# Block attention and a wave MLP on one core: the transposed input of the last middle tile from TensorE and ScalarE, its store on two queues

## Chip, core and metric

One core of a Trainium2 chip runs the kernel. The metric is the device time of one execution in microseconds; before the change its median is 190.77 us over three runs (190.2 to 191.58).

Five engines work side by side, each on its own instructions in order: TensorE (PE in the profile; PEld are its weight loads), VectorE (DVE), ScalarE (ACT), GpSimd (POOL) and SyncE (SP). They wait for each other by semaphores. DMAs are issued from the queues of SP, ACT and POOL and run on 16 shared DMA engines. A DMA issue stands in its engine's order like any instruction: what stands behind it, or ahead of it, is held up by it or holds it up.

## What is computed

```python
# q, k, v: 8 batches, 8 heads, 576 rows, 64 columns
scores = scale * q_c @ k_c.T            # in 9 chunks of 64 rows, each on its own
attn   = softmax(scores)
x      = attn @ v_c                     # heads side by side: x is [8, 576, 512]
theta  = x @ w_theta                    # [512, 512]
y      = einsum('ts,bsd->btd', w_tok_r, x * cos(theta)) \
       + einsum('ts,bsd->btd', w_tok_i, x * sin(theta))   # [576, 576] each
u      = x + y
out    = u + max(u @ w_ch, 0)           # w_ch is [512, 512], out float32
```

## The kernel before

The eight batches are taken as four pairs p = 0 to 3. A pair has 2 x 576 rows: four full tiles of 128 rows for each batch (j = 0 to 3 and j = 4 to 7) and one middle tile, j = 8, which holds the last 64 rows of both batches (MID in the code). So there are 36 tiles. Inside, everything is in fp16, with sums in fp32 in PSUM, which is one tile of eight banks.

The program is a list of steps in one string, ORDER (lines 17 to 64). Each step is written kind.tile.slot, and the loop at line 641 emits the steps one after the other. Nothing reorders them: on every engine the instructions stand in the order of the list, and only the waits between engines are put in by the framework, from the tiles that are written and read. The two digits of a step's tile are the pair and j, so 38 is the middle tile of the last pair, and 37 is its last full tile. The number behind it is a PSUM bank or the slot of a buffer.

The steps that the last 15 us are made of:

- Y.38.4 (line 523): the token mix of tile 38 on TensorE into bank 4. A.38 (line 550): VectorE adds x to it and writes u over x. Same for the other tiles.
- ud.38.3 (line 560, the DMA at line 565): u transposed into slot 3 of buffer uT by a DMA transpose on SyncE's queue. The other way, which the kernel uses for earlier tiles, is U.xx (line 554): four TensorE transposes of 128x128 into a bank, and ua.xx (line 569): ScalarE copies the bank into a slot of uT.
- W.38.5 (line 575): four matmuls of uT with w_ch into bank 5. W0 and W1 are halves of 256 columns, used for tile 37.
- R.38.0 (line 588): VectorE takes max(.,0), adds u, and writes slot 0 of the output buffer o. R0 and R1 are the halves.
- st, sa, sg (line 600): the store of a tile from o to the output, on the queue of SyncE, ScalarE or GpSimd. A middle tile goes to two batches and so is stored by two DMAs of 64 rows (line 605); a full tile by one (line 608). sx is a kind that puts the first half on SyncE's queue and the second on ScalarE's; ORDER does not use it before the change.

A slot of a buffer is written again only when its last reader is done. For o the reader is a store, and it is done when it has landed. The slots of o at the end: R.35.1, R.33.1 and R0.37.1 follow each other in slot 1; R.31.2, R.27.2 and R1.37.2 in slot 2; R.34.0 and R.38.0 in slot 0; R.30.3 and R.24.3 in slot 3. In uT, ud.38.3 follows ud.34.3.

The last steps on each engine, in order, before the change:

- TensorE: Y.38, W.34, W.36, W.30, W.33, W.27, W.32, W.38, W.24, W0.37, W1.37
- VectorE: A.37, R.35, R.31, A.38, R.34, R.30, R.36, R.33, R.27, R.32, R.38, R.24, R0.37, R1.37
- ScalarE: sa.28 (two DMAs), sa.35, sa.34, sa.33, sa.27, sa.24, sa1.37. It has no arithmetic after 155.2 us.
- SyncE: ud.36, ud.32, ud.27, ud.37, ud.38, st.30, st.38 (two DMAs), st0.37
- GpSimd: sg.31, sg.22, sg.36, sg.32

Of the kernel before, what the change touches and what calls it, by code (L numbers as in the profile page):

```python
# [14 lines left out]


ORDER = """
pre.00 hq.0A.0 hk.0A.1 lt.00.2 cqa.0A.3 ckv.0A Tq.0A.0 init.00 Tk1.0A Tk0.0A dm.28.7
S0.0A.0 S1.0A.2 lt.01.4 qk.0M.5 E0.0A.0 v.0A dm.15.7 V0.0A.4 E1.0A Tq.0M.1 Tk.0M qk.0B.6
V1.0A.6 N0.0A S.0M.0 N1.0A cta.01 Tq.0B.2 E.0M.1 v.0M cta.00 dm.6.3 X1.0A.2 Tk0.0B  # L20
X0.0A.3 dm.2.7 S0.0B.4 Tk1.0B V0.0M.0 xa0.0A.0 V1.0M.1 xa1.0A N0.0M E0.0B.2 S1.0B.6
E1.0B H0.0A.3 v.0B V1.0B.4 G0.0A.0 V0.0B.6 lw.01.7 H1.0A.2 N1.0M N1.0B X.0M.0 xa.0M.1
lw.03.8 N0.0B TW.01.4 twv.01 X1.0B.1 X0.0B.3 lw.02.9 xv0.0B.2 lw.00.10 G1.0A Z0.0A Z1.0A
xa1.0B H.0M.6 G.0M.1 H0.0B.7 TW.03.4 G0.0B.2 H1.0B.0 twv.03 G1.0B Z.0M Z0.0B qk.0C.11
Ya.01.3 v.0C Z1.0B TW.02.1 qk.0D.12 Ya.03.6 twa.02 Tq.0C.0 TW.00.4 Ym.05.7 Tk.0C v.0D
Ya.02.0 Yb.02 twv.00 S.0C.1 Ym.02 A.02 Yb.01 E.0C.3 Ym.01 V1.0C.4 A.01 V0.0C.0 Tq.0D.1
N1.0C Yb.03 lc.00 Ya.00.2 U.02.3 Tk.0D Yb.00 Ym.00 S.0D.4 N0.0C ua.02.0 A.00 X.0C.3
U.00.0 U.01.1 Ym.03 E.0D.0 xv.0C.3 uv.01.1 V1.0D.4 ua.00.2 N1.0D V0.0D.2 N0.0D qk.1M.0
qk.1A.1 H.0C.0 v.1M qk.1B.3 A.03 v.1A Ym.06.4 X.0D.5 W.02.2 Ym.07.3 xv.0D.0 G.0C.0 Z.0C
H.0D.5 Ya.05 Ya.06 Ya.07 G.0D.1 T.1M.2 S.1M.0 T.1A.0 Z.0D R.02.0 S.1A.5 E.1A.1 Yb.05  # L30
Yb.06 Ym.04.2 A.05 E.1M.2 V0.1M.5 N0.1M qk.1D.5 V1.1M.6 V1.1A.0 A.06 N1.1M Ya.04 T.1B.1
Yb.07 U.06.7 ua.06.3 A.07 X.1M.5 Yb.04 xa.1M.1 S.1B.6 N1.1A lw.04.4 TW.04.4 twv.04
H.1M.3 A.04 v.1B V0.1A.0 E.1B.3 V1.1B.4 G.1M.2 qk.2A.2 V0.1B.6 N0.1A N0.1B N1.1B Y.08.2
A.08 X.1A.0 W.00.1 U.04.6 qk.1C.6 X.1B.7 xa.1A.2 R.00.1 qk.2M.7 Z.1M T.1D.2 xa.1B.3
qk.2B.8 v.1D U.08.3 ua.08.4 v.2M v.1C ua.04.5 H.1A.4 G.1A.0 st.02 H.1B.0 W.08.2 W.06.7
U.05.3 T.1C.0 S.1D.4 G.1B.1 qk.2C.9 Z.1A Z.1B ua.05.6 E.1D.0 S.1C.0 W.01.6 R.06.2 U.07.3
sa.06 E.1C.2 T.2A.1 ua.07.7 Y.12.7 V1.1D.4 R.01.3 V0.1D.0 Y.13.6 T.2M.2 N0.1D S.2M.0
sa.01 E.2M.1 R.08.4 N1.1D S.2A.2 V1.1C.4 E.2A.3 sa.08 V0.1C.0 A.12 Y.11.7 X.1D.2 xa.1D.0
N1.1C N0.1C X.1C.3 xv.1C.1 Y.10.4 A.13 H.1D.0 qk.3M.10 v.2B T.2C.0 A.11 A.10 T.3M.2
G.1D.2 Z.1D H.1C.2 W.04.5 R.04.5 U.03.6 W.05.7 S.2C.0 v.2A st.00 S.3M.4 uv.03.0 G.1C.0  # L40
Z.1C R.05.0 E.3M.0 v.3M E.2C.2 st.04 V1.2A.2 N1.2A W.03.6 R.03.1 T.2B.1 Y.16.7 A.16
V0.2M.4 N0.2M v.2C V1.2C.2 V1.2M.5 qk.3A.11 N1.2C S.2B.0 N1.2M E.2B.1 qk.2D.12 Y.18.6
V1.3M.7 V0.2C.0 A.18 N0.2C V0.2B.2 N0.2B Y.14.4 V1.2B.5 V0.2A.0 qk.3C.0 v.2D N1.2B
U.18.2 Y.15.3 X.2B.5 A.14 X.2M.6 W.07.4 uv.18.2 xa.2B.2 N0.2A xa.2M.3 A.15 X.2A.2 v.3B
xa.2A.0 H.2B.0 T.3C.0 R.07.2 T.2D.2 G.2B.1 qk.3B.1 W.18.3 R.18.3 H.2A.5 U.15.4 Y.17.2
U.10.3 H.2M.0 Z.2B G.2A.2 ua.15.4 ua.10.3 N1.3M G.2M.0 S.3C.5 Z.2A A.17 S.2D.3 E.2D.2
W.15.1 U.17.7 Z.2M Y.20.2 uv.17.1 V1.2D.3 E.3C.1 A.20 V0.3M.0 V0.2D.5 st.05 Y.23.7
xd.2C.1 N1.2D A.23 N0.2D T.3B.1 U.14.2 U.11.3 sa.18 N0.3M xd.2D.2 W.17.4 ua.11.5 U.16.7
R.15.4 st.07 Y.21.3 A.21 R.17.5 qk.3D.3 v.3C v.3A H.2C.5 ua.16.6 T.3A.0 W.10.7 ua.14.0
G.2C.1 T.3D.2 H.2D.0 G.2D.2 Y.22.2 Z.2C R.10.0 S.3D.3 S.3A.5 st.15 E.3A.3 S.3B.0 E.3D.0  # L50
Z.2D Y.26.7 sg.03 U.12.5 A.22 U.13.2 sa.10 ua.13.7 W.11.6 R.11.3 Y.25.3 A.26 E.3B.2 v.3D
sa.11 ud.23.2 ud.21.4 W.16.4 A.25 R.16.1 W.13.2 V1.3D.0 R.13.2 V1.3A.6 V0.3A.3 N1.3D
ua.12.1 N0.3A st.16 sa.13 xd.3M.0 N1.3A Y.24.5 A.24 Y.27.2 A.27 W.12.0 R.12.4 V0.3D.3
V1.3B.6 V0.3B.1 N1.3B xd.3A.3 ud.20.3 N0.3B N0.3D Y.28.5 V1.3C.6 V0.3C.0 A.28 W.14.2
H.3M.3 G.3M.0 R.14.0 xd.3B.1 ud.25.5 N0.3C H.3A.4 xd.3D.2 G.3A.1 W.21.2 N1.3C R.21.3
W.23.0 Z.3A H.3B.6 G.3B.2 sg.17 Z.3M ud.24.6 W.25.1 sa.21 R.23.5 xd.3C.0 H.3D.2 ud.28.7
W.20.4 H.3C.5 ud.22.1 G.3D.1 R.25.1 Z.3B Y.30.0 G.3C.0 Z.3D ud.26.0 sg.12 Z.3C Y.31.7
R.20.2 A.30 A.31 Y.36.1 Y.35.2 W.22.3 A.35 R.22.4 Y.33.5 W.28.6 A.33 Y.34.4 sg.23 A.34
ud.35.4 R.28.3 ud.31.2 W.26.0 Y.32.7 Y.37.2 W.35.3 A.36 ud.33.5 R.26.5 W.31.5 A.32 A.37
Y.38.4 ud.34.3 ud.30.1 st.26 ud.36.7 sa.20 sg.25 sa.28 R.35.1 R.31.2 ud.32.0 A.38  # L60
ud.27.4 sg.14 W.34.6 W.36.1 W.30.0 W.33.7 sg.31 sa.35 R.34.0 ud.37.2 ud.38.3 R.30.3
st.30 W.27.2 sa.34 R.36.5 sg.22 R.33.1 sg.36 R.27.2 W.32.3 R.32.4 W.38.5 R.38.0 sg.32
sa.33 sa.27 W.24.4 R.24.3 sa.24 W0.37.6 R0.37.1 st.38 W1.37.0 R1.37.2 sa1.37 st0.37
""".split()


# [611 lines left out]
```

## Time and profile before

| what | value |
|---|---|
| median of three runs | 190.77 us |
| the profiled execution, its own time | 190.93 us |
| span of its profile, first to last instruction | 189.2 us |
| granted TensorE clock, mean | 0.994 |
| stores at the end: last one issued, landed after | 184.70 us, 3.3 us |

The times in the profile count from the first instruction, so they stand against the span of 189.2 us; the execution's own time is 1.7 us longer. A row of the timeline has the start, the length, the engine, the line, the operation, what it writes and reads, its shape, and how many instructions are merged into it; brackets at its end give how long the engine was idle before and what ended that. A q behind an engine's name marks its sequencer, which issues DMAs. The length of a DMA row is that of its issue; when it landed is told by the DMA issues (line, queue, count, KB each, median us from issue to landing). Busy shares are averages over the whole span; what one change is worth is read at its place in the timeline and in the chain of work that ended last.

### The profile page before, as it was taken

The page shows a single profiled execution, that of the slowest core. Times are in us where ns is not written, and L with a number is a line of the kernel's source. Part 1 is how long each engine was busy: PE and PEld are TensorE (multiplying, and loading weights), DVE is VectorE, ACT ScalarE, POOL GpSimd, SP SyncE. Part 2 cuts the span into 40 slices and gives each one's busy share as a digit, 9 for nine tenths or more (in the row PEclk, how much of TensorE's full clock was granted, in tenths as well). Part 3 has the DMA queues.
Part 4 walks back from the last instruction along what each step waited for, and adds up shares of the span by engine and source line. Part 5 has one row for each costly group of instructions (what it writes and reads, how often), then busy time and mean ns, then how long its engine had stood idle before and what let it go on. Part 6 is the DMA issues. An engine that isn't in the chain of part 4 may idle for free.

```text
span 189.2 us, 6104 instructions
## 1 busy us (share of the span) xinstructions
PE 180.9 (96%) x2645; PEld 93.4 (49%) x2645; DVE 136.7 (72%) x259; ACT 94.8 (50%) x123; POOL 89.5 (47%) x129
## 2 busy tenths in 40 slices
PE   7998999999999999999999999999999999999970
PEld 2455555554566465545564555464554444444430
DVE  0426887889798999699887858945797963464760
ACT  3246996186566993586229966694306660000000
POOL 8765996689795885899359440100010200002010
PEclk9999999999999999999999999999999999999997
DMA  5999999999999999999999996911467851257986
GB/s 151 285 194 172 177 167 170 189 168 168 192 194 180 198 126 206 178 101 191 209 166 146 172 214 52 248 60 59 140 153 154 183 177 59 55 110 204 206 317 166
DMA packets 99227, 31.48 MB, mean 166 GB/s; under 512 B 90880, under 2 KB 94848, under 8 KB 99200
## 3 DMA queue, kind: packets, MB, share of 16 engines
q0 software_dynamic: 75952, 18.11, 99.2%
q1 hardware_dynamic: 20896, 8.92, 21.2%
q10 hardware_dynamic: 2352, 4.06, 6.7%
q8 instruction: 20, 0.33, 0.7%
q14 instruction: 7, 0.06, 0.1%
HBM read 33.06 MB, written 9.44 MB: 225 GB/s over the span
## 4 chain that ended last, share of the span: by engine, by line
PE 74%; DMA 17%; DVE 3%; issue 2%; POOL 2%; SPq 0%; DVEq 0%; POOLq 0%
PE psum L540 34%; PE psum L475 15%; PE psum L580 12%; DMA land<-in_k_dram 9%; PE psum L354 4%; PE psum L400 3%; DMA land<-in_q_dram 3%; DMA uT<-x 3%; PE psum L437 2%; PE psum L557 2%; DMA v<-in_v_dram 2%; PE psum L287 2%; POOL v L213 1%; DVE o L592 1%; DVE T L335 1%
## 5 line engine op out<-in xcount | busy, mean ns | idle before, releaser
L213 POOL DMA_DIRECT2D v<-in_v_dram x56 | 41.7, 765 | 14.5 <-DMA land<-in_k_dram 9.1
L540 PEld LDWEIGHTS <-wT 128*128 128x128 f16 (+1 forms) x360 | 30.6, 100 | 33.4 <-issue 0.8
L540 PE MATMUL psum<-zr,wT 128*128 128x512 f16 (+1 forms) x180 | 45.4, 381 | 0.1
L540 PE MATMUL psum<-zi,wT 128*128 128x512 f16 (+1 forms) x180 | 43.1, 379 | 0.0
L608 POOL DMA_DIRECT2D out_dram<-o x10 | 5.5, 552 | 66.3 <-DVE o L592 46.2
L580 PE MATMUL psum<-wch,uT 128*128 128x512 f16 (+1 forms) x148 | 35.2, 374 | 1.1 <-DMA uT<-x 1.1
L552 DVE TENSOR_TENSOR x<-psum,x 128x512 f16<-128x512 f32 x36 | 24.4, 683 | 15.8 <-PE psum L540 15.1
L475 PE MATMUL psum<-wtheta,xT 128*128 128x512 f16 x144 | 34.1, 379 | 0.0
L592 DVE SCALAR_TENSOR_TENSOR o<-psum,x 128x512 f32<-128x512 f32 (+1 forms) x37 | 24.3, 670 | 10.3 <-PE psum L580 6.2
L494 ACT ACTIVATE cos<-psum,pihalf 128x1024 f16<-128x1024 f32 (+1 forms) x22 | 21.2, 964 | 16.1 <-PE psum L475 16.1
L335 DVE STREAM_TRANSPOSE T<-land 64x256 f32<-64x256 f32 (+3 forms) x38 | 27.0, 725 | 2.6 <-DMA land<-in_k_dram 2.3
L417 DVE TENSOR_TENSOR x<-psum,recip 128x512 f16<-128x512 f32 (+1 forms) x40 | 25.5, 638 | 1.4
L383 ACT ACTIVATE eT<-psum 128x1024 f16<-128x1024 f32 (+1 forms) x22 | 18.4, 864 | 15.8 <-PE psum L354 15.8
L580 PEld LDWEIGHTS <-uT 128*128 128x128 f16 x148 | 13.7, 98 | 16.2 <-DMA uT<-x 1.6
L475 PEld LDWEIGHTS <-xT 128*128 128x128 f16 x144 | 13.5, 98 | 15.3 <-DVE xT L460 0.2
L143 ACT ACT_TABLE_LOAD x14 | 18.0, 1283 | 4.1 <-DVE recip L415 3.1
L494 ACT ACTIVATE sin<-psum 128x1024 f16<-128x1024 f32 (+1 forms) x22 | 19.1, 870 | 0.0
L173 POOL DMA_DIRECT2D land<-in_q_dram x15 | 13.6, 904 | 4.8 <-DVE recip L415 2.1
L157 PE MATMUL psum<-zeros 128*128 128x512 f16 x51 | 14.1, 436 | 1.2 <-DVE pihalf L148 1.2
L173 POOL DMA_DIRECT2D land<-in_k_dram x15 | 13.5, 902 | 2.0 <-DMA land<-in_k_dram 1.4
L462 ACT COPY xT<-psum 128x512 f16<-128x512 f16 (+1 forms) x11 | 8.4, 784 | 10.4 <-PE psum L437 10.4
L354 PEld LDWEIGHTS <-T 32*64 32x64 f16 x1152 | 10.6, 105 | 5.4 <-DVE T L335 2.1
(40 smaller groups left out, 140.9 us busy)
## 6 DMA issues: line engine op xcount, KB each, us to landing
land<-in_q_dram POOLq DMA_DIRECT2D x15, 256.0 KB, 6.8
land<-in_k_dram POOLq DMA_DIRECT2D x15, 256.0 KB, 7.8
out_dram<-o ACTq DMA_DIRECT2D x12, 256.0 KB, 3.2
v<-in_v_dram POOLq DMA_DIRECT2D x40, 64.0 KB, 6.2
out_dram<-o POOLq DMA_DIRECT2D x10, 256.0 KB, 3.4
out_dram<-o SPq DMA_DIRECT2D x9, 256.0 KB, 3.3
v<-in_v_dram POOLq DMA_DIRECT2D x16, 128.0 KB, 7.7
land<-in_moe_w_theta_dram SPq DMA_DIRECT2D x2, 512.0 KB, 7.6
```

Source lines behind the costliest of these rows:

```text
L173: nc.gpsimd.dma_start(t[:, w].rearrange("p h s d -> p h (s d)"), ap[2 * p + bb, :, s0 : s0 + GT, :].rearrange("h (p s) d -> p h (s d)", s=2),)
L213: nc.gpsimd.dma_start(v16[rows, slot + t, :, 0:D], v[b, :, t0 : t0 + m, :].rearrange("h s d -> s h d"),)
L335: nc.vector.transpose(to.bitcast(FP32).rearrange("p (x l s) -> p x s l", l=32, s=2), src.bitcast(FP32).rearrange("p (x s d) -> p x s d", s ...
L354: nc.tensor.matmul(ps[half[rows], r, h - hs[0]], t[quarter[c], 1, h, :, e], t[quarter[c], 0, h, :, e], start=(e == 0), stop=(e == 1), tile ...
L383: nc.scalar.activation(out=to, in_=ps, func=AF.Exp, scale=scale)
L417: nc.vector.tensor_tensor(out=x.rearrange("p r (h d) -> p r h d", h=H // 2), in0=ps[:, :, :, 0:D], in1=recip[:, 0:n].broadcast_to((P, n, H ...
L475: nc.tensor.matmul(ps[:, (j - js[0]) * DM : (j - js[0] + 1) * DM], xT[:, j, a, :], wtheta16[:, a, :], start=(a == 0), stop=(a == NDB - 1),)
L494: nc.scalar.activation(out=t[:, js[0] : js[-1] + 1].rearrange("p j e -> p (j e)"), in_=ps, func=AF.Sin, bias=bias, scale=1.0,)
L540: nc.tensor.matmul(ps[half[c]] if j == MID else ps, wT[:, kt, t0 : min(t0 + P, S)], z, start=(b is not None and i == 0), stop=(i == len(kt ...
L552: nc.vector.tensor_tensor(out=x, in0=st.pop(("ps_y", p, j)), in1=x, op=ALU.add)
L580: nc.tensor.matmul(ps, uT[:, a, :], wch16[:, a, cols[f]], start=(a == 0), stop=(a == NDB - 1),)
L592: nc.vector.scalar_tensor_tensor(out=o, in0=ps, scalar=0.0, in1=st["x", p][:, j, cols[f]], op0=ALU.max, op1=ALU.add,)
```

## The change

Four steps of ORDER differ. ud.38.3 goes; U.38.2 (four transposes into bank 2) and ua.38.3 (ScalarE's copy into the same slot of uT) come in ahead of W.30, which is also ahead of sa.35 on ScalarE. st.38 goes; sx.38 comes in ahead of W.24 in the list, with the first half on SyncE's queue and the second on ScalarE's, behind sa.27 and ahead of sa.24. All else is the same; the string is wrapped anew, so line numbers are three less from there on. The core of the diff, with the list's lines as they are wrapped:

```diff
...
-ud.27.4 sg.14 W.34.6 W.36.1 W.30.0 W.33.7 sg.31 sa.35 R.34.0 ud.37.2 ud.38.3 R.30.3
-st.30 W.27.2 sa.34 R.36.5 sg.22 R.33.1 sg.36 R.27.2 W.32.3 R.32.4 W.38.5 R.38.0 sg.32
-sa.33 sa.27 W.24.4 R.24.3 sa.24 W0.37.6 R0.37.1 st.38 W1.37.0 R1.37.2 sa1.37 st0.37
...
+Y.37.2 W.35.3 A.36 ud.33.5 R.26.5 W.31.5 A.32 A.37 Y.38.4 ud.34.3 ud.30.1 st.26 ud.36.7 sa.20
+sg.25 sa.28 R.35.1 R.31.2 ud.32.0 A.38 ud.27.4 sg.14 W.34.6 W.36.1 U.38.2 ua.38.3 W.30.0 W.33.7
+sg.31 sa.35 R.34.0 ud.37.2 R.30.3 st.30 W.27.2 sa.34 R.36.5 sg.22 R.33.1 sg.36 R.27.2 W.32.3
+R.32.4 W.38.5 R.38.0 sg.32 sa.33 sa.27 sx.38 W.24.4 R.24.3 sa.24 W0.37.6 R0.37.1 W1.37.0 R1.37.2
+sa1.37 st0.37
```

More of the change, by code (lines that the diff above doesn't have):

```diff
@@ L17 @@
 ORDER = """
[L18 to L59, printed above, removed]
@@ L60 @@
-Y.38.4 ud.34.3 ud.30.1 st.26 ud.36.7 sa.20 sg.25 sa.28 R.35.1 R.31.2 ud.32.0 A.38
-ud.27.4 sg.14 W.34.6 W.36.1 W.30.0 W.33.7 sg.31 sa.35 R.34.0 ud.37.2 ud.38.3 R.30.3
-st.30 W.27.2 sa.34 R.36.5 sg.22 R.33.1 sg.36 R.27.2 W.32.3 R.32.4 W.38.5 R.38.0 sg.32
-sa.33 sa.27 W.24.4 R.24.3 sa.24 W0.37.6 R0.37.1 st.38 W1.37.0 R1.37.2 sa1.37 st0.37
+pre.00 hq.0A.0 hk.0A.1 lt.00.2 cqa.0A.3 ckv.0A Tq.0A.0 init.00 Tk1.0A Tk0.0A dm.28.7 S0.0A.0
+S1.0A.2 lt.01.4 qk.0M.5 E0.0A.0 v.0A dm.15.7 V0.0A.4 E1.0A Tq.0M.1 Tk.0M qk.0B.6 V1.0A.6 N0.0A
@@ new lines @@
+S.0M.0 N1.0A cta.01 Tq.0B.2 E.0M.1 v.0M cta.00 dm.6.3 X1.0A.2 Tk0.0B X0.0A.3 dm.2.7 S0.0B.4
+Tk1.0B V0.0M.0 xa0.0A.0 V1.0M.1 xa1.0A N0.0M E0.0B.2 S1.0B.6 E1.0B H0.0A.3 v.0B V1.0B.4 G0.0A.0
+V0.0B.6 lw.01.7 H1.0A.2 N1.0M N1.0B X.0M.0 xa.0M.1 lw.03.8 N0.0B TW.01.4 twv.01 X1.0B.1 X0.0B.3
+lw.02.9 xv0.0B.2 lw.00.10 G1.0A Z0.0A Z1.0A xa1.0B H.0M.6 G.0M.1 H0.0B.7 TW.03.4 G0.0B.2 H1.0B.0
+twv.03 G1.0B Z.0M Z0.0B qk.0C.11 Ya.01.3 v.0C Z1.0B TW.02.1 qk.0D.12 Ya.03.6 twa.02 Tq.0C.0
+TW.00.4 Ym.05.7 Tk.0C v.0D Ya.02.0 Yb.02 twv.00 S.0C.1 Ym.02 A.02 Yb.01 E.0C.3 Ym.01 V1.0C.4
@@ new lines @@
+A.01 V0.0C.0 Tq.0D.1 N1.0C Yb.03 lc.00 Ya.00.2 U.02.3 Tk.0D Yb.00 Ym.00 S.0D.4 N0.0C ua.02.0
+A.00 X.0C.3 U.00.0 U.01.1 Ym.03 E.0D.0 xv.0C.3 uv.01.1 V1.0D.4 ua.00.2 N1.0D V0.0D.2 N0.0D
+qk.1M.0 qk.1A.1 H.0C.0 v.1M qk.1B.3 A.03 v.1A Ym.06.4 X.0D.5 W.02.2 Ym.07.3 xv.0D.0 G.0C.0 Z.0C
+H.0D.5 Ya.05 Ya.06 Ya.07 G.0D.1 T.1M.2 S.1M.0 T.1A.0 Z.0D R.02.0 S.1A.5 E.1A.1 Yb.05 Yb.06
+Ym.04.2 A.05 E.1M.2 V0.1M.5 N0.1M qk.1D.5 V1.1M.6 V1.1A.0 A.06 N1.1M Ya.04 T.1B.1 Yb.07 U.06.7
+ua.06.3 A.07 X.1M.5 Yb.04 xa.1M.1 S.1B.6 N1.1A lw.04.4 TW.04.4 twv.04 H.1M.3 A.04 v.1B V0.1A.0
@@ new lines @@
+E.1B.3 V1.1B.4 G.1M.2 qk.2A.2 V0.1B.6 N0.1A N0.1B N1.1B Y.08.2 A.08 X.1A.0 W.00.1 U.04.6 qk.1C.6
+X.1B.7 xa.1A.2 R.00.1 qk.2M.7 Z.1M T.1D.2 xa.1B.3 qk.2B.8 v.1D U.08.3 ua.08.4 v.2M v.1C ua.04.5
+H.1A.4 G.1A.0 st.02 H.1B.0 W.08.2 W.06.7 U.05.3 T.1C.0 S.1D.4 G.1B.1 qk.2C.9 Z.1A Z.1B ua.05.6
+E.1D.0 S.1C.0 W.01.6 R.06.2 U.07.3 sa.06 E.1C.2 T.2A.1 ua.07.7 Y.12.7 V1.1D.4 R.01.3 V0.1D.0
+Y.13.6 T.2M.2 N0.1D S.2M.0 sa.01 E.2M.1 R.08.4 N1.1D S.2A.2 V1.1C.4 E.2A.3 sa.08 V0.1C.0 A.12
+Y.11.7 X.1D.2 xa.1D.0 N1.1C N0.1C X.1C.3 xv.1C.1 Y.10.4 A.13 H.1D.0 qk.3M.10 v.2B T.2C.0 A.11
@@ new lines @@
+A.10 T.3M.2 G.1D.2 Z.1D H.1C.2 W.04.5 R.04.5 U.03.6 W.05.7 S.2C.0 v.2A st.00 S.3M.4 uv.03.0
+G.1C.0 Z.1C R.05.0 E.3M.0 v.3M E.2C.2 st.04 V1.2A.2 N1.2A W.03.6 R.03.1 T.2B.1 Y.16.7 A.16
+V0.2M.4 N0.2M v.2C V1.2C.2 V1.2M.5 qk.3A.11 N1.2C S.2B.0 N1.2M E.2B.1 qk.2D.12 Y.18.6 V1.3M.7
+V0.2C.0 A.18 N0.2C V0.2B.2 N0.2B Y.14.4 V1.2B.5 V0.2A.0 qk.3C.0 v.2D N1.2B U.18.2 Y.15.3 X.2B.5
+A.14 X.2M.6 W.07.4 uv.18.2 xa.2B.2 N0.2A xa.2M.3 A.15 X.2A.2 v.3B xa.2A.0 H.2B.0 T.3C.0 R.07.2
+T.2D.2 G.2B.1 qk.3B.1 W.18.3 R.18.3 H.2A.5 U.15.4 Y.17.2 U.10.3 H.2M.0 Z.2B G.2A.2 ua.15.4
@@ new lines @@
+ua.10.3 N1.3M G.2M.0 S.3C.5 Z.2A A.17 S.2D.3 E.2D.2 W.15.1 U.17.7 Z.2M Y.20.2 uv.17.1 V1.2D.3
+E.3C.1 A.20 V0.3M.0 V0.2D.5 st.05 Y.23.7 xd.2C.1 N1.2D A.23 N0.2D T.3B.1 U.14.2 U.11.3 sa.18
+N0.3M xd.2D.2 W.17.4 ua.11.5 U.16.7 R.15.4 st.07 Y.21.3 A.21 R.17.5 qk.3D.3 v.3C v.3A H.2C.5
+ua.16.6 T.3A.0 W.10.7 ua.14.0 G.2C.1 T.3D.2 H.2D.0 G.2D.2 Y.22.2 Z.2C R.10.0 S.3D.3 S.3A.5 st.15
+E.3A.3 S.3B.0 E.3D.0 Z.2D Y.26.7 sg.03 U.12.5 A.22 U.13.2 sa.10 ua.13.7 W.11.6 R.11.3 Y.25.3
+A.26 E.3B.2 v.3D sa.11 ud.23.2 ud.21.4 W.16.4 A.25 R.16.1 W.13.2 V1.3D.0 R.13.2 V1.3A.6 V0.3A.3
@@ new lines @@
+N1.3D ua.12.1 N0.3A st.16 sa.13 xd.3M.0 N1.3A Y.24.5 A.24 Y.27.2 A.27 W.12.0 R.12.4 V0.3D.3
+V1.3B.6 V0.3B.1 N1.3B xd.3A.3 ud.20.3 N0.3B N0.3D Y.28.5 V1.3C.6 V0.3C.0 A.28 W.14.2 H.3M.3
+G.3M.0 R.14.0 xd.3B.1 ud.25.5 N0.3C H.3A.4 xd.3D.2 G.3A.1 W.21.2 N1.3C R.21.3 W.23.0 Z.3A H.3B.6
+G.3B.2 sg.17 Z.3M ud.24.6 W.25.1 sa.21 R.23.5 xd.3C.0 H.3D.2 ud.28.7 W.20.4 H.3C.5 ud.22.1
+G.3D.1 R.25.1 Z.3B Y.30.0 G.3C.0 Z.3D ud.26.0 sg.12 Z.3C Y.31.7 R.20.2 A.30 A.31 Y.36.1 Y.35.2
+W.22.3 A.35 R.22.4 Y.33.5 W.28.6 A.33 Y.34.4 sg.23 A.34 ud.35.4 R.28.3 ud.31.2 W.26.0 Y.32.7
```

## The prediction

> **What bounds the kernel now.** I read the page's busy shares first, then the chain of work that ended last, then the timeline of TensorE and of the queues from 172 us on, and last the DMA issues with their times to landing.
>
> ```profile
> PE 180.9 (96%) x2645; PEld 93.4 (49%) x2645; DVE 136.7 (72%) x259; ACT 94.8 (50%) x123; POOL 89.5 (47%) x129
> ...
> PE 74%; DMA 17%; DVE 3%; issue 2%; POOL 2%; SPq 0%; DVEq 0%; POOLq 0%
> ```
>
> TensorE is busy for 96% of the span, so a gain must take work from it or close one of its few gaps. Its last gap is in the end of the chain (start, length, what):
>
> ```profile
> 176.01 5.32 DMA uT<-x
> 181.33 0.05 issue
> 181.37 1.91 PE psum L580 x8
> 183.29 0.02 issue
> 183.31 0.06 DVE o L592
> 183.37 0.39 issue
> 183.76 0.05 DVEq L592
> 183.81 0.11 issue
> 183.92 0.41 DVE o L592
> ```
>
> The transfer is ud.38, the DMA transpose that the change removes: issued at 176.01, landed at 181.33. TensorE starts W.38 0.04 us later. The timeline of TensorE gives the size of the gap:
>
> ```profile
> 174.92 5.35 PE L580 MATMUL psum<-wch,uT 128*128 128x512 f16 x24
> 181.37 2.77 PE L580 MATMUL psum<-wch,uT 128*128 128x512 f16 x16 [1.10 <-DMA uT<-x]
> ```
>
> The 24 matmuls are W.34, W.36, W.30, W.33, W.27, W.32, four each. The 16 are W.38, W.24 and the halves of W.37. The row of 24 lasts 5.35 us with 0.38 for the last matmul, so the matmuls follow each other every 0.216 us. Without a wait W.38 would start at 174.92 + 24 x 0.216 = 180.11: the wait moves it by 1.26 us. The last rows of the kernel are the two halves of tile 37: R1.37 and its store sa1.37.
>
> ```profile
> 184.25 0.42 DVE L592 SCALAR_TENSOR_TENSOR o<-psum,x 128x256 f32<-128x256 f32 x1
> 184.70 0.41 ACTq L608 DMA_DIRECT2D out_dram<-o  x1
> out_dram<-o ACTq DMA_DIRECT2D x1, 128.0 KB, 3.3
> ```
>
> So the end is 184.70 + 3.3 = 188.0 and then 1.2 us of closing to 189.2. Whatever moves R1.37 moves the end.
>
> **The change, part by part. U.38 on TensorE.** Four transposes of 128x128 are added between W.36 and W.30. No row shows them at that place; U steps elsewhere do (two U steps in one row, the matmul behind them, and the copy on ScalarE):
>
> ```profile
> 127.41 0.61 PE L557 MATMUL psum<-id,x 128*128 128x128 f16 x8
> 127.86 1.03 PE L580 MATMUL psum<-wch,uT 128*128 128x512 f16 x4
> 128.06 0.59 ACT L569 COPY uT<-psum 128x512 f16<-128x512 f16 x1 [0.80 <-PE psum L557]
> ```
>
> Eight take 127.86 - 127.41 = 0.45, so four take 0.23 us. U.38 starts after W.36, at 174.92 + 8 x 0.216 = 176.65. It needs x of tile 38 from A.38:
>
> ```profile
> 175.03 0.69 DVE L552 TENSOR_TENSOR x<-psum,x 128x512 f16<-128x512 f32 x1 [1.38 <-PE psum L540]
> ```
>
> That ends at 175.72, 0.9 before it is needed, and bank 2 was last read by A.37, before A.38. So no wait. W.30, W.33, W.27 and W.32 each start 0.23 later.
>
> **ua.38 on ScalarE.** In the row above the copy starts 0.65 us after the first transpose of its row of eight, which is 0.42 for a row of four; it lasts 0.59. So it runs from 177.07 to 177.66. W.27 needs bank 2 back at 174.92 + 16 x 0.216 + 0.23 = 178.61: 0.95 to spare. W.38 can start at 180.11 + 0.23 = 180.34: 2.7 to spare. TensorE gains 181.37 - 180.34 = 1.03 us, if nothing else holds it. The banks of W.38, W.24 and W.37 were read out before 178.7 (R.30 is the last of them), so no bank does.
>
> **What is queued behind ua.38.** ScalarE's queue is in order, and behind ua.38 stands sa.35, the store of tile 35, which did not have to wait for TensorE before. These are the stores on that queue now, with VectorE's R.33 and R.27:
>
> ```profile
> 172.82 0.34 ACTq L608 DMA_DIRECT2D out_dram<-o  x1
> ...
> 176.72 0.37 ACTq L608 DMA_DIRECT2D out_dram<-o  x1
> ...
> 179.64 0.34 ACTq L608 DMA_DIRECT2D out_dram<-o  x1
> ...
> 180.23 0.34 ACTq L608 DMA_DIRECT2D out_dram<-o  x1
> ```
>
> ```profile
> 178.92 0.68 DVE L592 SCALAR_TENSOR_TENSOR o<-psum,x 128x512 f32<-128x512 f32 x1
> ...
> 179.52 0.68 DVE L592 SCALAR_TENSOR_TENSOR o<-psum,x 128x512 f32<-128x512 f32 x1
> ```
>
> They are sa.35, sa.34, sa.33, sa.27; then R.33, R.27. A DMA that stands behind a ScalarE instruction is issued 0.07 us after that one starts:
>
> ```profile
> 147.92 1.11 ACT L494 ACTIVATE cos<-psum,pihalf 128x1024 f16<-128x1024 f32 x1 [1.43 <-PE psum L475]
> 147.99 0.34 ACTq L608 DMA_DIRECT2D out_dram<-o  x1
> ```
>
> So sa.35 goes from 172.82 to 177.14, 4.3 us later, and sa.34 follows at about 177.5 instead of 176.72. This has a price, through the output buffers. R.35.1 and R.33.1 share o slot 1, so R.33 may not write before sa.35 has landed. R0.37.1 uses that slot again and waits for sa.33; R1.37.2 uses slot 2 and waits for sa.27. The landing times of sa.35, of sa.34, and of sa.33 with sa.27, in this order:
>
> ```profile
> out_dram<-o ACTq DMA_DIRECT2D x1, 256.0 KB, 2.6
> ...
> out_dram<-o ACTq DMA_DIRECT2D x1, 256.0 KB, 4.4
> ...
> out_dram<-o ACTq DMA_DIRECT2D x2, 256.0 KB, 3.4
> ```
>
> Before, sa.35 landed at 175.4, 3.5 us ahead of R.33. Now its landing is bounded by 2.6 (its own row) and 4.4 (sa.34, issued nearly at the new moment, but beside ud.38, which is gone). I take 2.6: beside it only ud.37 is left. It lands at 179.75 and R.33 starts at 179.8, where TensorE and R.36 alone would allow 178.92 + 0.23 = 179.15.
>
> sa.27 is issued 180.23 - 178.92 = 1.31 after R.33 starts, so at 181.1. Its landing is bounded by 2.6 and 3.4. The stretches of the DMA engines tell why it took 3.4 (last two columns: share and GB/s):
>
> ```profile
> 178.40:179.00 0.60, 0.60 (x4) 0.28 (x3) 0.60 (x3) 0.00 (x0) 0.00 (x0) 1.00 0.24 9
> 179.00:180.30 1.30, 1.27 (x6) 0.39 (x4) 1.20 (x3) 0.00 (x0) 0.54 (x1) 1.00 1.02 200
> 180.30:183.40 3.10, 2.03 (x11) 1.06 (x12) 1.47 (x3) 0.00 (x0) 0.54 (x1) 1.00 1.05 408
> ```
>
> While the two late transposes hung, only 9 GB/s moved, and then the stores filled the engines at 408 GB/s for 3 us. After the change half of that jam is gone, but sa.35's 256 KB are added, so I take the middle, 3.0: sa.27 lands at 184.1. R1.37 then starts at 184.1 instead of 184.25, where TensorE alone would allow about 184.25 - 1.03 = 183.2. The ring of output buffers hands back 0.9 of the 1.03.
>
> The Trainium skill (DMA: Bandwidth & Descriptors, Anatomy of one DMA) fits 2.0 us plus bytes over 436 GB/s to a DMA. By it a 256 KB store is an estimated 2.6 us, as sa.35's row has it and the 3.4 and 4.4 rows do not; the second rival is the case in which the trace would agree with it.
>
> **The store in two halves.** The two halves of st.38 leave one queue, and st0.37 stands behind them:
>
> ```profile
> 183.17 1.19 SPq L605 DMA_DIRECT2D out_dram<-o  x2
> 184.46 0.53 SPq L608 DMA_DIRECT2D out_dram<-o  x1
> ```
>
> Moved to ScalarE's queue, the second half costs it about 0.6 us (1.19 / 2) between sa.27 and sa.24. R.38 ends 0.6 before R.24 on VectorE (the distance of R.33 and R.27), so sa.24 goes when R.24 is done, within 0.1. SyncE's queue gets 0.6 us back ahead of st0.37, which started 0.13 after R0.37's end (183.92 + 0.41). That isn't the last store; sa1.37 is. I cost this part at nothing, from -0.1 (st0.37) to +0.1 (sa.24 pushing sa1.37). The Trainium skill (DMA: Bandwidth & Descriptors, Issuing engines are not separate DMA queues) says that issuing from several engines saves the sequencer's issue time alone; the 0.6 is that, and by it too the sum stays.
>
> **ud.38 off SyncE's queue.** Behind it stands st.30, which waits for R.30 anyway (at 178.44, 0.9 after ud.38's issue ended). It moves with R.30 by 0.23: nothing. POOL's queue (sg.36, sg.32) moves with VectorE and ends before the others. No instruction ahead of W.34 is changed.
>
> **The sum** on the profiled execution: TensorE -1.26 + 0.23 = -1.03; ring of buffers +0.88; store 0; last landing 3.3 as before. That is -0.15: 190.93 - 0.15 = 190.8 there. The median of the runs, 190.77, is 0.16 below the profiled run, so 190.6.
>
> **The rivals.** (1) The gain reaches the end. For: landings of 2.4 to 2.6 where the engines are free (sa.35, and the jam is smaller). R.33 goes at 179.5, sa.27 at 180.8, lands at 183.3; R1.37 gains 0.95. Against: seven stores of 256 KB in 5 us. 189.8.
> (2) Every store lands unloaded, 2.6 for 256 KB (sa.35's row) and 2.4 for the last one, the least that a store on SyncE's queue took (st.26's row):
>
> ```profile
> out_dram<-o SPq DMA_DIRECT2D x1, 256.0 KB, 2.4
> ```
>
> R1.37 starts at 179.8 + 1.31 + 2.6 = 183.7, 0.55 earlier, and the last landing is 0.9 shorter: 189.3. Against: sa.33 and sa.27 at 3.4, sa1.37 at 3.3. The skill's fit, above, is the page that speaks for it.
> (3) Slower: sa.35 is late. With 4.4 us it lands at 181.55; R.33 starts then, sa.27 goes at 182.86 and lands, by 3.4, at 186.25: R1.37 is 2.0 later, 192.8; with 3.4 and 3.4 it is 1.0 later, 191.8. It decides from a landing of about 2.8 on (179.95 + 1.31 + 3.0 = 184.26, where it was). For: sa.34 at 176.72. Against: ud.38, the later of two transposes beside that store, is gone.
> (4) W.38 still waits, because U.38 or ua.38 does. For it A.38 would have to be 0.9 late, or the copy 2.7. Then the time is 190.8 or more.
>
> **How the numbers follow.** Forecast 0.5; rival 1 0.23; rival 2 0.07; rival 3 0.17; rival 4 0.03. The predicted time is the forecast's, 190.6. Its own part runs from 190.2 to 191.2. The range goes from 189.5 (inside rival 1, above rival 2) to 192.2 (the middle of rival 3) and leaves out 2 in 10. A measurement of this kernel can tell about 1% (1.9 us) from no change. Faster by that means under 188.9: below every case, 0.03. Slower means above 192.7: the top of rival 3, 0.05. Within 1%: 0.92.
>
> **What would show it.** Right: no TensorE gap ahead of W.38, and W.38 starting near 180.3; four L557 rows near 176.65 and one copy near 177.1; sa.35 at about 177.1 behind it; a VectorE gap of 0.3 to 1.0 ahead of R.33; another gap ahead of the halves of R.37, ended by the landing of sa.33 or sa.27 and not by TensorE. Wrong: R.33 starting at 179.15 with sa.35 landed (rival 1), all landings under 2.7 (rival 2), R.33 after 180.3 (rival 3), a gap ahead of W.38 (rival 4). The whole working would fall if something ahead of 174.9 moved.

## The result, and the profile after

The changed kernel takes 192.2 us (median; 191.66 to 193.66) against 190.68 before: a ratio of 1.0086 with a 95% interval of 1.0057 to 1.0115, or 1.1 to 2.2 us slower. The forecast was 190.6 and no measurable change. The time is within 1% of before, as forecast, but the change can be measured: the interval is 0.3% to either side, where the prediction had taken 1%.

The profiled execution took 193.66 us, the longest of the changed kernel's, with a span of 191.6. Its times are best read from the start of W.34, the first of the last matmuls, which lies at 174.92 before and at 177.28 here. This is TensorE's timeline after (start, length, operation, count), from W.34 on:

```profile
177.28 1.90 PE L577 MATMUL psum<-wch,uT 128*128 128x512 f16 x8
179.02 0.39 PE L554 MATMUL psum<-id,x 128*128 128x128 f16 x4
179.24 6.22 PE L577 MATMUL psum<-wch,uT 128*128 128x512 f16 x32
```

The gap ahead of W.38 is gone: after the four transposes 32 matmuls run without a stop, and W.30 starts 1.96 after W.34, as the prediction's 176.65 + 0.23 has it (176.88 is 1.96 after 174.92). From W.34 to the end, however, it takes 191.64 - 177.28 = 14.36 us, against 14.24 before; this stretch is called the tail from here on. The copy and the first store behind it, in ScalarE's timeline:

```profile
179.44 0.58 ACT L566 COPY uT<-psum 128x512 f16<-128x512 f16 x1 [21.95 <-PE psum L554]
179.50 0.34 ACTq L605 DMA_DIRECT2D out_dram<-o  x1
```

sa.35 is issued 2.22 after W.34 (prediction: 177.14, the same 2.22) instead of 2.10 ahead of it. It lands 3.0 us later:

```profile
out_dram<-o ACTq DMA_DIRECT2D x1, 256.0 KB, 3.0
```

VectorE shows who waits for that: R.34, then R.30 and R.36, then R.33 and all that follow.

```profile
178.35 0.69 DVE L589 SCALAR_TENSOR_TENSOR o<-psum,x 128x512 f32<-128x512 f32 x1 [0.27 <-PE psum L577]
180.30 1.29 DVE L589 SCALAR_TENSOR_TENSOR o<-psum,x 128x512 f32<-128x512 f32 x2 [1.26 <-PE psum L577]
182.57 3.97 DVE L589 SCALAR_TENSOR_TENSOR o<-psum,x 128x512 f32<-128x512 f32 x7 [0.98 <-DMA out_dram<-o]
```

R.33 starts 5.29 after W.34 (4.00 before), behind a gap of 0.98 that a store ends, not TensorE. R.33 and the six behind it then stand in one row, with TensorE ahead of them.

The chain of work that ended last runs the same way, from the transposes to the copy, ScalarE's queue, a store and VectorE:

```profile
179.18 0.24 PE psum L554 x4
...
179.44 0.02 ACT uT L566
...
179.50 0.34 ACTq L605
...
179.93 3.11 DMA out_dram<-o
...
183.18 2.26 DVE o L589 x4
...
185.57 0.43 DVE o L589
...
186.11 0.42 DVE o L589
```

The chain takes the later store, sa.34 (issued at 179.93), because a wait for it stands in VectorE's stream and came last. VectorE's own rows show that the block had begun at 182.57, with the landing of sa.35 at 182.45; sa.34 landed at 183.04, in time for R.38 at 184.4. R1.37 starts at 186.11, 8.84 after W.34 (9.33 before). The last three stores, sa.24, st0.37 and sa1.37, took 3.1, 3.1 and 3.3 us to land before; the first two take longer now:

```profile
out_dram<-o ACTq DMA_DIRECT2D x1, 256.0 KB, 3.3
out_dram<-o SPq DMA_DIRECT2D x1, 128.0 KB, 3.6
out_dram<-o ACTq DMA_DIRECT2D x1, 128.0 KB, 3.3
```

So the last landing is 12.6 after W.34, against 13.1 in the first profile of before.

There is one more thing at the very end that the prediction does not have. Behind the last landing SyncE passes its closing waits one by one. The last five of them, before and after (count, durations, first and last start):

```profile
L673 SPq EVENT_SEMAPHORE  x5: 28/28/28, 188.0 to 188.3; - x5
```

```profile
L670 SPq EVENT_SEMAPHORE  x5: 28/28/28, 190.0 to 190.7; - x5
```

Five waits that passed in 0.3 us now take 0.7, though no landing is left to wait for: the last one is at 189.9. Between the second and the third SyncE stands still for 0.46 us. The span ends 1.74 us after the last landing, before 1.17.

### The profile page after: what moved, and what is told of

Same layout as the page of the kernel before. It is cut to its first block, busy times and chain, and to the rows that moved or that the text cites. A ratio compares the mean times of both kernels' runs of the same rounds, so it can differ in the third digit from the quotient of the medians.

```text
span 191.6 us, 6113 instructions
## 1 busy us (share of the span) xinstructions
PE 181.1 (95%) x2649; PEld 93.5 (49%) x2649; DVE 136.9 (71%) x259; ACT 95.5 (50%) x124; POOL 89.5 (47%) x129
## 4 chain that ended last, share of the span: by engine, by line
PE 73%; DMA 12%; DVE 6%; POOL 4%; issue 2%; ACTq 0%; DVEq 0%; POOLq 0%; ACT 0%
PE psum L537 33%; PE psum L472 15%; PE psum L577 11%; DMA v<-in_v_dram 7%; DMA land<-in_k_dram 4%; PE psum L351 4%; PE psum L397 3%; DVE o L589 2%; PE psum L434 2%; PE psum L554 2%; POOL land L165 2%; DMA out_dram<-o 2%; PE psum L284 2%; DVE T L332 1%; DVE x L549 1%
## 5 line engine op out<-in xcount | busy, mean ns | idle before, releaser
L566 ACT COPY uT<-psum 128x512 f16<-128x512 f16 x15 | 8.5, 592 | 32.5 <-PE psum L554 31.5
L472 PEld LDWEIGHTS <-xT 128*128 128x128 f16 x144 | 13.5, 98 | 15.2 <-DVE xT L457 0.2
L577 PEld LDWEIGHTS <-uT 128*128 128x128 f16 x148 | 13.8, 98 | 14.6 <-issue 0.4
L170 POOL DMA_DIRECT2D land<-in_q_dram x15 | 13.8, 918 | 3.8 <-DVE x L414 1.3
L170 POOL DMA_DIRECT2D land<-in_k_dram x15 | 13.8, 918 | 1.3 <-DMA land<-in_k_dram 0.7
```

The lines of the kernel that those rows point to most:

```text
L170: nc.gpsimd.dma_start(t[:, w].rearrange("p h s d -> p h (s d)"), ap[2 * p + bb, :, s0 : s0 + GT, :].rearrange("h (p s) d -> p h (s d)", s=2),)
L472: nc.tensor.matmul(ps[:, (j - js[0]) * DM : (j - js[0] + 1) * DM], xT[:, j, a, :], wtheta16[:, a, :], start=(a == 0), stop=(a == NDB - 1),)
L577: nc.tensor.matmul(ps, uT[:, a, :], wch16[:, a, cols[f]], start=(a == 0), stop=(a == NDB - 1),)
```

## The experiments

All times are medians of runs on the same chip beside runs of the kernel before (191.3 to 191.45 us there, so ratios are compared). "After W.34" means after the start of the first matmul of W.34. Where a run is set beside the changed kernel, its ratio is set beside the 1.0061 of the changed kernel's second run, unless another is named. That run and the three experiments behind it were on one chip, all later ones on another.

**The changed kernel again.** No edit.

> The changed kernel, unaltered, for a second profile and more times. Its first profile starts W.34 at 177.28 us, 2.36 later than before (174.92), though no instruction ahead of W.34 differs; from W.34 to the end of the span it takes 14.3, before 14.2. Theory A (the loss is in the tail: ua.38 holds sa.35 up, sa.35 holds R.33 up, and so on to the halves of tile 37; the 2.36 us are chance): W.34 starts at 174.9 plus or minus 0.8 here, and R.33 again starts about 5.3 after W.34 with a gap of 0.7 to 1.3 ahead of it. Theory B (the loss lies ahead of W.34 and comes with the changed program): W.34 starts 1 us or more late again, and the tail is as long as before. Time 191.7 to 192.7 in both.

Measured: 192.34 us, ratio 1.0061 (1.0034 to 1.0088). W.34 started at 177.24, as late as in the first profile; R.33 5.13 after W.34 with a gap of 0.82; tail 14.4. The tail answers theory A, the start of W.34 theory B. The start alone does not settle it: both profiled executions were the longest of their kernel (193.49 here, of 191.34 to 193.49), so their late start need not be that of the median run.

**sa.35 ahead of the copy.**

```diff
-W.34.6 W.36.1 U.38.2 ua.38.3 W.30.0 W.33.7 sg.31 sa.35
+W.34.6 W.36.1 sa.35 U.38.2 ua.38.3 W.30.0 W.33.7 sg.31
```

> The changed kernel with sa.35 moved ahead of U.38 and ua.38 in the list, so that ScalarE issues it as early as before. Theory A: sa.35 starts about 2.1 before W.34, R.33 has no gap ahead of it and starts 4.2 after W.34; the halves of tile 37 start 0.4 to 1.0 earlier than in the changed kernel; time 0.5 to 1.2 below the changed kernel, 191.0 to 191.7. Theory B: R.33's gap goes too, but the time is within 0.3 of the changed kernel's. Theory C (the second half of the store on ScalarE's queue makes the end late): within 0.3 of the changed kernel.

Measured: 191.93 us, ratio 1.0026 (1.0000 to 1.0053), 0.35% below the changed kernel; the two intervals overlap, and the medians differ by 0.4 us where theory A expected 0.5 to 1.2. VectorE:

```profile
178.86 3.28 DVE L589 SCALAR_TENSOR_TENSOR o<-psum,x 128x512 f32<-128x512 f32 x5 [1.26 <-PE psum L577]
```

R.30 to R.32 run as a block of five again. W.34 starts at 175.84, so R.33 starts 4.23 after it, R1.37 8.41 (8.84 in the changed kernel), and the tail is 13.8 instead of 14.4. Theory A holds for 0.5 us of the tail. It isn't all: the kernel is still not faster than before.

**Only the transposes and the copy; the store as before.**

```diff
-sa.33 sa.27 sx.38 W.24.4 R.24.3 sa.24 W0.37.6 R0.37.1 W1.37.0
+sa.33 sa.27 W.24.4 R.24.3 sa.24 W0.37.6 R0.37.1 st.38 W1.37.0
```

> The changed kernel with tile 38 stored as before, both halves on SyncE's queue (only the transposes and the copy are new). Theory C: 0.4 to 1.2 faster than the changed kernel, near 191.0 to 191.8. Theory A: within 0.3 of the changed kernel, 192.0 to 192.5. Theory B: within 0.3 as well.

Measured: 192.57 us, ratio 1.0086 (1.0052 to 1.0120), as slow as the changed kernel or slower; tail 14.9. Theory C falls. The loss comes with the transposes, the copy and the removal of ud.38. In the tail the store in halves even gains here: without it st0.37 is issued behind both halves of tile 38 and lands last, 13.1 after W.34, where the changed kernel's last landing is at 12.6. This is one profile against two, and the time does not tell the two apart.

**Only the store in two halves.**

```diff
-sa.33 sa.27 W.24.4 R.24.3 sa.24 W0.37.6 R0.37.1 st.38 W1.37.0
+sa.33 sa.27 sx.38 W.24.4 R.24.3 sa.24 W0.37.6 R0.37.1 W1.37.0
```

> The kernel before with only the store of tile 38 in two halves on two queues. Theory A: within 0.3 of before, 190.4 to 191.0. Theory C: 0.4 to 1.2 slower than before, 191.1 to 191.9. Theory B (any change of the program moves the part ahead of W.34): W.34 starts late and the time rises by 0.5 or more.

Measured: 190.81 us, ratio 0.9977 (0.9957 to 0.9998). This half of the change does no harm. Its profile brought the next question: W.38, which still waits for ud.38 here, started only 5.63 after W.34, not 6.45.

**The kernel before again.** No edit.

> The kernel before, unaltered, for a second profile. Theory F (the first profile of before was not a usual one: ud.38 landed unusually late, so removing it is worth less than 1.03): W.38 starts 5.4 to 5.9 after W.34 instead of 6.45, and from W.34 to the end of the span it takes 13.3 to 13.9 instead of 14.2. If the first profile was usual, W.38 starts 6.3 to 6.6 after W.34 and the tail is 14.1 to 14.4. The first matmul of W.34 starts between 174.5 and 177 by chance. Time within 0.4 of before.

Measured: 191.0 us, ratio 0.9989 (0.9959 to 1.0019). TensorE from W.34 on:

```profile
175.84 5.35 PE L580 MATMUL psum<-wch,uT 128*128 128x512 f16 x24
181.38 2.77 PE L580 MATMUL psum<-wch,uT 128*128 128x512 f16 x16 [0.19 <-DMA uT<-x]
```

The same gap that took 1.10 us in the first profile takes 0.19 here. W.38 starts 5.54 after W.34, where 24 matmuls without a wait end at 5.19: removing ud.38 is worth 0.35 less the 0.23 of the transposes. The tail is 13.34, not 14.24: W.38 is 0.91 earlier and the tail 0.90 shorter. Theory F holds.

**A longer stream for SyncE.**

```diff
-sa.06 ... sa.01 ... sa.08
+st.06 ... st.01 ... st.08
```

> The changed kernel with three early stores (tiles 06, 01, 08) issued by SyncE instead of ScalarE, which makes SyncE's stream some instructions longer; nothing after 110 us differs. In the four kernels without ud.38 SyncE stops for 0.43 us among its closing waits, always behind the same number of its instructions, and the end comes 1.74 after the last landing; in the two with ud.38 it comes 1.17 after. Theory D (the stop sits at a fixed place of SyncE's stream, which is shorter without ud.38): the stop moves ahead to where SyncE waits for a landing anyway, the end comes 1.2 after the last landing, time 0.3 to 0.7 below the changed kernel. Theory A alone, without D: the end stays 1.74 after the last landing and the time is within 0.3 of the changed kernel's.

Measured: 191.67 us, ratio 1.0023 (0.9997 to 1.0050), 0.38% below the changed kernel, with overlapping intervals. R.33 still waits (5.21 after W.34), and the tail is 13.9 instead of 14.4. SyncE's stop of 0.46 us is there, but further ahead: it ends at 187.51, and the last landing is at 187.47, so it hides behind that. The span ends 1.36 after the last landing. Counted in the trace, it again stands behind the 79th instruction of SyncE, as in every other kernel that shows it. SyncE has 87 instructions in the changed kernel, 91 in this one and in the kernel before.

**A shorter stream for SyncE, ud.38 kept.** An edit of the kernel before.

```diff
-st.02 ... st.00 ... st.04
+sa.02 ... sa.00 ... sa.04
```

> The kernel before with three early stores (tiles 02, 00, 04) issued by ScalarE instead of SyncE, so that SyncE's stream is about as short as in the changed kernel, with ud.38 still there. Theory D: a stop of 0.4 appears among SyncE's closing waits, the end comes 1.6 to 1.8 after the last landing instead of 1.17, time 0.2 to 0.7 above before. If the stop belongs to the absence of ud.38 and not to the length of the stream: the end stays 1.17 after the last landing, time within 0.3 of before.

Measured: 191.05 us, ratio 0.9998 (0.9968 to 1.0028). The closing waits:

```profile
L670 SPq EVENT_SEMAPHORE  x5: 28/28/28, 187.9 to 188.6; - x5
```

The stop is there behind the 79th of 87 instructions, with ud.38 in place, and the span ends 1.65 after the last landing. So the stop goes with the length of SyncE's stream and not with ud.38, as theory D has it. The time does not show it: the interval takes in a rise of 0.5 us, but the median does not rise, and the expected 0.2 to 0.7 is not shown. What the three stores moved to ScalarE give back is not known.

**A slot of its own for R.33.**

```diff
-R.33.1
+R.33.6
```

> The changed kernel with R.33 writing a slot of its own in the output buffer, so that it need not wait for sa.35; sa.35 stays behind ua.38. Theory A: no gap ahead of R.33, which starts 4.2 after W.34 instead of 5.1 to 5.3; R1.37 starts 0.3 to 0.6 earlier (8.3 to 8.5 after W.34 instead of 8.7 to 8.8); time 0.2 to 0.8 below the changed kernel. If the late sa.35 costs in another way than through slot 1 (the stores crowd at the end): R1.37 moves by less than 0.2 and the time stays within 0.3.

Measured: 191.52 us, ratio 1.0017 (0.9990 to 1.0044), 0.44% below the changed kernel, with overlapping intervals. sa.35 stays behind the copy, and still:

```profile
179.38 3.28 DVE L589 SCALAR_TENSOR_TENSOR o<-psum,x 128x512 f32<-128x512 f32 x5 [1.26 <-PE psum L577]
```

With W.34 at 176.36 R.33 starts 4.23 after it and R1.37 8.42, as with sa.35 ahead; the tail is 13.9. It is slot 1 through which the late store costs: freeing the slot gives the same R.33, R1.37 and tail as issuing sa.35 early.

**Both costs taken away.** The changed kernel with sa.35 ahead of U.38 and the three early stores on SyncE's queue.

> The changed kernel with sa.35 ahead of U.38 and ua.38, and with three early stores on SyncE's queue: the late R.33 and the stop among the closing waits are both taken away, the transposes and the copy stay. Theory A with D and F: R.33 starts 4.2 after W.34, the last landing is 12.0 to 12.2 after W.34, the end 1.2 to 1.4 behind it; the tail of 13.2 to 13.6 is that of the kernel before in its usual state (13.34 in its second profile), so the time is within 0.3% of before. If the removal of ud.38 is worth its 1.0 us once those two are gone: 0.4% or more faster than before. If a further loss belongs to the transposes or lies ahead of W.34: 0.3% or more slower.

Measured: 190.80 us, ratio 0.9970 (0.9943 to 0.9997). VectorE has no gap ahead of R.33 (the row starts with R.30 and R.36):

```profile
178.86 3.28 DVE L589 SCALAR_TENSOR_TENSOR o<-psum,x 128x512 f32<-128x512 f32 x5 [1.26 <-PE psum L577]
```

R.33 starts 4.23 after W.34, the last landing is 12.3 after it (12.0 to 12.2 was expected), and the span ends 1.24 behind that; tail 13.5. Once more:

> The kernel with both costs of the change taken away, once more, because it came out 0.3% faster than before with an interval that almost reaches 1. If that holds, the ratio is 0.995 to 0.999; if it was chance, 0.999 to 1.002. R.33 starts 4.2 after W.34, the end comes 1.2 to 1.4 after the last landing.

Measured: 190.87 us, ratio 0.9982 (0.9951 to 1.0014), tail 13.1. The transposes with both costs off are no slower than the kernel before, and 0.2 to 0.3% faster at the medians; one of the two intervals includes 1. Both runs also have the store in halves, whose ratio alone was 0.9977, so no gain is shown for the transposes. Both intervals lie below those of the changed kernel (from 1.0034 and 1.0057 on): the two edits together take the whole loss away, which neither does clearly in time alone.

**The store in halves again.**

> The kernel before with only the store of tile 38 in two halves on two queues, once more, to see whether its 0.2% holds: R.38's two halves start together, st0.37 is no longer behind two issues; last landing 12.0 to 12.2 after W.34, ratio 0.996 to 1.000. If the 0.2% was chance, the ratio is 1.000 or above.

Measured: 191.45 us, ratio 0.9983 (0.9953 to 1.0014). The ratio is 0.2% below 1 again, but the median is not below the 191.36 of the runs beside it: a gain of 0.2% cannot be told from none.

**The kernel before, a third time.**

> The kernel before, a third profile. Theory F: W.38 starts 5.5 to 6.2 after W.34 (5.54, 5.63 and 6.20 in the other three kernels that keep ud.38, 6.45 in the first profile, 5.19 without a wait). A start of 6.4 or more would make the first profile the usual one. Ratio 0.998 to 1.002.

Measured: 191.32 us, ratio 0.9990 (0.9967 to 1.0013). The gap ahead of W.38 is so small that the 40 matmuls stand in one row:

```profile
176.37 8.27 PE L580 MATMUL psum<-wch,uT 128*128 128x512 f16 x40
```

It takes 8.27; the changed kernel takes 8.18 for the same 40 with the transposes among them (from 177.28 to 179.24 + 6.22). W.38 starts 5.50 after W.34. In the six profiles that keep ud.38 it starts at 5.35, 5.50, 5.54, 5.63, 6.20 and 6.45; the one on which the prediction was built is the last.

## Why the prediction was wrong, point by point

**The size of the wait.** "The wait moves it by 1.26 us" was read rightly from one profile and was the longest of six. In the two other profiles of the same kernel it is 0.35 and 0.31. So the gain of TensorE was not 1.03 but about 0.1. This is the first term of the sum that failed, by its size and not by its mechanism: where W.38 was 0.91 later, the tail was 0.90 longer. About 0.1 holds for the two usual profiles; two of the six start W.38 late, and against the mean of all six, 5.78, the 5.41 of the changed kernel is a gain of 0.4. The wait varied from 0.16 to 1.26 us over the six profiles, while the 24 matmuls ahead of it took 5.35 us in each profile that shows them as one row.

**U.38 and ua.38.** Right in place and size: 0.22 us of TensorE, copy 2.16 after W.34, no wait for A.38, for bank 2 or for a slot.

**sa.35 behind the copy, and the ring of output buffers.** Right as a mechanism: sa.35 2.22 after W.34, the gap ahead of R.33, the store that ends it. The sizes were off both ways: sa.35 took 2.95 to land and not 2.6, and R.33 started at 5.29 instead of 4.88; sa.27 took 2.1 and not 3.0, so R1.37 started at 8.84 instead of 9.18. That it costs is shown twice in the tail, by moving sa.35 and by freeing the slot: 0.5 us each time. In time the two are 0.35% and 0.44% below the changed kernel, each by itself at the edge of what the runs can tell. The forecast had charged 0.88 for the ring against a gain of 1.03; against a gain of 0.1, the 0.5 that it cost is nearly all loss.

**ud.38 off SyncE's queue.** "It moves with R.30 by 0.23: nothing" missed the second lost term. SyncE has 87 traced instructions instead of 91; three of the four went with ud.38 (88 with the transposes alone) and one with the second half of the store (90 with that alone). With that, a stop of 0.46 us comes to stand behind the last landing. In the kernels with 88 or 87 the span ends 1.65 to 1.78 after the last landing, in those with 90 or 91 it ends 1.17 to 1.36 after it. In the kernel before a wait for a landing stands in that place, so whether the stop is there too, hidden, can only be inferred. That it stands at a fixed place of the stream is shown by its moving along when the stream is made longer or shorter, with ud.38 and without. In the tail it costs 0.57. In time the kernel with the longer stream points to it (0.38% below the changed one, with overlapping intervals); the one with the shorter stream does not. No run moves the early stores without moving the stop, so what these moves do to the time by themselves is not known.

**The store in two halves.** Forecast at nothing, between -0.1 and +0.1; the ratios are 0.2% below 1 in both trials, one interval just below 1 and one not. The sign was within reach, the size is at the edge of what can be told.

**The sum as it is.** In the tail: 13.3 (the kernel before in its second profile), + 0.5 (ring), + 0.57 (stop), less 0.1 (TensorE) is 14.3; 14.4 was seen in both profiles of the changed kernel. That is + 1.0 us of the 1.2 to 1.6 us that the two ratios give (0.61% and 0.86%); 1.0 lies inside the interval of the second (0.65 to 1.7 us) and just below that of the first (1.1 to 2.2 us). From the changed kernel's tail of 14.4, taking the ring's cost away leaves 13.8 and 13.9, hiding the stop 13.9, and both 13.5 and 13.1, so the two add up. Rival 3 named the right side and the right queue, but its price of 1.0 to 2.0 came from a landing of 3.4 to 4.4 that did not occur; that the loss came out near it is chance.

**What stays open.** W.34 started at 177.28 and 177.24 in the two profiles of the changed kernel and between 174.92 and 176.37 in the kernels that keep ud.38. Nothing ahead of W.34 differs. About half of the 2.36 us between the first profiles of before and after is one gap on TensorE. It is shown here after and in the second profile of the kernel before; the first has none:

```profile
94.08 0.41 PE L537 MATMUL psum<-zi,wT 128*64 128x512 f16 x2 [1.09 <-issue]
```

```profile
92.64 0.41 PE L540 MATMUL psum<-zi,wT 128*64 128x512 f16 x2 [0.48 <-issue]
```

The gap is always ahead of the same matmul: 1.09 and 1.25 us in the two profiles of the changed kernel, 0.12 to 0.92 in nine others, none in three. What it waits for is not shown. In the other kernels with the transposes W.34 starts between 174.94 and 176.36, as without them, so nothing ahead of W.34 belongs to the transposes as such. Whether the changed kernel itself has a little of it in its median run is not known: 0.2 to 0.6 us of its loss are not accounted for by the tail, or are noise.

## What to carry to other kernels

A gain that is the length of a wait for a DMA should be read from more than one execution before it is booked; the length of an instruction can be read from one. Work that is put on an engine's queue holds up the stores that stand behind it, and a late store comes back as a late write into the buffer that it empties: follow the slot numbers, and either issue the ready store first or give the next writer another slot. An instruction taken from a queue also moves everything behind it in that queue's stream, and a stop that hid in a wait can come out at the end.

## What the runs showed of the hardware

SyncE stands still for 0.46 us behind the same count of its own instructions (79 in the trace) in the nine profiles that show it. In the other five a wait for a landing, 0.58 to 0.82 us long, stands in that place. That it is the fetch of instructions is a guess; no view names it.

With plain stores and DMA transposes under way together, all DMA engines can come nearly to rest. First the changed kernel, where sa.35 and sa.34 start beside ud.37; then the kernel with sa.35 ahead, at the same distance from W.34 and just before that (the last three columns are TensorE's clock, the DMA engines' share and GB/s):

```profile
180.30:181.00 0.70, 0.70 (x5) 0.33 (x4) 0.70 (x2) 0.00 (x0) 0.00 (x0) 1.00 1.17 53
```

```profile
178.85:179.55 0.70, 0.70 (x5) 0.32 (x4) 0.69 (x2) 0.00 (x0) 0.00 (x0) 1.00 0.97 314
```

```profile
178.40:178.85 0.45, 0.45 (x3) 0.20 (x2) 0.00 (x0) 0.18 (x1) 0.00 (x0) 1.00 0.68 61
```

At a share near 1 the engines move 53 GB/s in the one and 314 in the other, so the share does not tell how much they move. The kernel with sa.35 ahead has its stretch of little transfer too, only shorter (61 GB/s for 0.45 us). The kernel before has one at 178.4 in the prediction's rows (9 GB/s, at a share of 0.24). There ud.38 and sa.34 are late together: sa.34 took 4.40 and 4.17 us to land in the two profiles with the late W.38, and 3.1 to 3.4 in the other four. What sets such a stretch off, how long it lasts, and on which transfer it falls was not tried; that the stores or the transposes cause it is not shown.

Set beside the Trainium skill (DMA: Bandwidth & Descriptors, Anatomy of one DMA), whose fit gives an estimated 2.6 us for 256 KB, the stores of 256 KB from sa.35 on took 2.1 to 3.3 us in the changed kernel: it lies in the middle, and the end of this kernel depends on the spread. The page made the fit for DMAs that GpSimd issues, while the prediction set it beside stores of ScalarE's queue; the two of these stores that GpSimd issued took 2.35 and 2.39 us.
